# GFNet spectral filter and gated FFN on one core: a reordered opening, and the middle spectral stage two places sooner

## The chip, the cores and the metric

The kernel runs on one core of a Trainium2 chip. The metric is the device time of one execution in microseconds; before the change the median of three runs is 193.73 (193.61 to 193.73).

## The reference

The input x has 2048 rows (tokens) of 640 in bf16; the FFN's inner width is F = 1536.

```
xn  = layernorm(x)                                   # no scale, no shift
s   = irfft2(rfft2(xn) * (w_r + 1j*w_i)).astype(bf16)   # over all 2048 x 640
g   = silu((gelu(xn @ w_gate) * (xn @ w_up)) @ w_down)
out = x + s * g
```

So there are two branches out of one normalized input, a spectral filter and a gated FFN, and they meet in the last line.

## The kernel before

**Tiles.** The 2048 tokens are 16 slabs of 128; four slabs are a group of 512 (g = 0 to 3). F is 12 tiles of 128. A slab is loaded (`load_x`), its mean and variance are taken by VectorE in two halves (`bn_half`, L189) and joined (`bn_join`, L195; `stats` is both), the inverse root comes from POOL (`root`, L207, a power, behind an addition on VectorE, L205) or for slab 0 from ScalarE (`root_act`, L214, followed on L215 by a small gelu that brings in the gelu table), and VectorE normalizes in place (`norm`, L218, or in two parts, `norm_parts`). Then TensorE turns the slab (`slab_Tparts`, L994, five transposes, three and two), and the turned slab is copied out of PSUM (L995), the first part by VectorE and the second by ScalarE. Slab 2 is turned by TensorE with one copy by ScalarE, and slabs 4 to 15 by DMA (`slab_T`, L532 and L539); for slabs 4 to 7 ScalarE normalizes (`norm_act`, L461) by a product that POOL prepares (`shift`, L456).

**FFN.** For one tile t and columns c0 to c1, `ffn_piece` (L826) does five matmuls with Wg, then gelu on ScalarE (L837), and five with Wu, then the product on VectorE (L839). PSUM has two banks for gate results and two for up results (`bank`), used in turn.

**The order is written out by hand.** The list `back` has 144 places, one after the other on TensorE. Group 0 has 16 opening places for tiles 0 to 7 (first slab by slab, then with 256 columns at a time), the eight places of tiles 8 to 11 with all 512 columns, and 12 places of the down projection. Groups 1 and 2 have 24 FFN places and 12 places of `product` (six matmuls of 128x320 each); group 3 has 24 FFN places and 12 down places. `plan[s]` holds what is issued behind the matmuls of place s, by `put(s, function, ...)`: statistics, norms, building of constants (`inv_consts` and `inv_rest`, L313 and L318; the phase tables on POOL, L334 to L374 and L386), and the spectral branch.

**The spectral branch.** Forward: folds on VectorE, `slab_S1` (L555) and `slab_D`, slab by slab from place 30 to 56, written to ZDR in DRAM. Middle: `s2_step` in 11 bursts from place `sb` = 67 on, with B loaded from ZDR (L603), a first transform (px, L628), the multiplication by the weights (L644), a second one (pu, L657), sorting by ScalarE and VectorE (L672), and writes to UDR. Inverse: from `sb` + 24 on, the loads of V, `slab_S1i`, `slab_Di`, and the combination with the FFN's result (`group_*`, `finish`). All of these places are worked out from `sb`.

**The opening.** SP's queue loads in this order: X 0, X 1, Wu 0:2, Wu 2:4, X 2, Wu 4:6, X 3, Wg and Wu 6:8, X 4:8, the weights 8:12 and the rest. ScalarE's queue loads Wg 0:2, 2:4 and 4:6 (L231, L232). TensorE runs 21 warm-up matmuls on ones (`warm_pe`, L588), the transposes of slab 0, two warm-ups more, and then place 0. VectorE does the statistics of slab 0 and of slab 1, and then the norm of slab 0.

Of the kernel before, what the change touches and what calls it, by code (L numbers as in the profile page):

```python
# [10 lines left out]
BF16 = mybir.dt.bfloat16  # L11
INT32 = mybir.dt.int32
ACT = mybir.ActivationFunctionType
ALU = mybir.AluOpType
P = 128
# [17 lines left out]
def kernel(  # L33
# [39 lines left out]
    with tc.manual_schedule():  # L73
        build(nc, locals())


def build(nc, env):
    consts, big, wts, work, psA, psB = (env[k] for k in ("consts", "big", "wts", "work", "psA", "psB"))
    ZDR, UDR, X, Wg, Wu, Wd, W1, W2 = (env[k] for k in ("ZDR", "UDR", "X", "Wg", "Wu", "Wd", "W1", "W2"))
# [3 lines left out]
    def load_x(n0, n, eng=nc.sync):  # L83
        eng.dma_start(out=X[:, n0:n0 + n, :], in_=xv[:, n0:n0 + n, :])

    def load_w(k, t0, t1, eng=nc.sync):
        f0, f1 = t0 * P, t1 * P
        eng.dma_start(out=(Wg, Wu)[k][:, :, f0:f1], in_=(wgv, wuv)[k][:, :, f0:f1])

    def load_gu(t0, t1):  # L90
        for k in range(2):
            load_w(k, t0, t1)

    load_x(0, 1)
    load_x(1, 1)
    load_w(1, 0, 2)
    load_w(1, 2, 4)
    load_x(2, 1)
    load_w(1, 4, 6)
    load_x(3, 1)  # L100
    load_gu(6, 8)
    load_x(4, 4)
    load_gu(8, 12)
    load_x(8, 4)
# [32 lines left out]
    UT = consts.tile([P, NT, 512], BF16, name="UT")  # L137
# [8 lines left out]
    def slot(k, *shape):  # L146
        return XG[:, k, :].rearrange("p (a b) -> p a b", b=shape[-1])
# [25 lines left out]
    def c1(name, dt=FP32):  # L173
        return consts.tile([P, 1], dt, name=name)

    done = set()
    mva = {}
    rstd = {}
    rall = {}
    nmr = {}  # L180
    xnT = {}
# [4 lines left out]
    def bn_half(n1, k):  # L186
        if k == 0:
            st_n[n1] = work.tile([P, 2, nc.vector.BN_STATS_DIM], FP32, tag="st", bufs=3, name="st")
        nc.vector.bn_stats(out=st_n[n1][:, k, :], in_=X[:, n1, 320 * k:320 * k + 320])  # L189

    def bn_join(n1):
        g = n1 // 4
        if g not in mva:
            mva[g] = work.tile([P, 4, nc.vector.BN_AGGR_DIM], FP32, tag="mva", bufs=2, name=f"mva{g}")
        nc.vector.bn_aggr(out=mva[g][:, n1 % 4, :], in_=st_n[n1])  # L195
# [6 lines left out]
    def root(n0, n):  # L202
        m = mva[n0 // 4][:, n0 % 4:n0 % 4 + n, :]
        ve = work.tile([P, 4], FP32, tag="ve", name="ve")[:, 0:n]
        nc.vector.tensor_scalar(out=ve, in0=m[:, :, 1], scalar1=1e-5, scalar2=None, op0=ALU.add)  # L205
        r = work.tile([P, 4], FP32, tag="rst", bufs=4, name="rst")[:, 0:n]
        nc.gpsimd.tensor_tensor(out=r, in0=ve, in1=mhalf[:, 0:n], op=ALU.pow)  # L207
        rall[n0] = r
        for k in range(n):
            rstd[n0 + k] = r[:, k:k + 1]  # L210

    def root_act(n1):
        rstd[n1] = c1("rst0")
        nc.scalar.activation(out=rstd[n1], in_=mva[n1 // 4][:, n1 % 4, 1:2], func=ACT.Abs_reciprocal_sqrt, bias=eps)  # L214
        nc.scalar.activation(out=warm, in_=negpi, func=ACT.Gelu_apprx_tanh)  # L215

    def norm(n1, c0=0, c1_=D):
        nc.vector.tensor_scalar(out=X[:, n1, c0:c1_], in0=X[:, n1, c0:c1_], scalar1=mva[n1 // 4][:, n1 % 4, 0:1],  # L218
                                scalar2=rstd[n1], op0=ALU.subtract, op1=ALU.mult)
        if c1_ == D:  # L220
            done.add(("n", n1))
# [6 lines left out]
    eps = c1("eps")  # L228
    nc.vector.memset(eps, 1e-5)
    nc.scalar.activation(out=warm, in_=eps, func=ACT.Abs_reciprocal_sqrt)  # L230
    for t in (0, 2, 4):  # L231
        load_w(0, t, t + 2, nc.scalar)  # L232
    b_0, b_1 = c1("b_0"), c1("b_1")
    nc.vector.memset(b_0, 320.0)
    nc.vector.memset(b_1, 0.0)
# [92 lines left out]
    stats(0)  # L328
    bn_half(1, 0)
    root_act(0)  # L330

    def tinv_phase(h):
# [251 lines left out]
    def warm_pe(n):  # L584
        if not warm_bank:
            warm_bank.append(bank(0))
        for _ in range(n):
            nc.tensor.matmul(warm_bank[0][:, 0:256], lhsT=ones[:, 0:P], rhs=ones, start=True, stop=True)  # L588
# [230 lines left out]
    def bank(k):  # L819
        return psA.tile([P, 512], FP32, tag="gu"[k], name="ps" + "gu"[k])  # L820

    cur = {}

    ges = {}

    def ffn_piece(g, t, k, c0, c1_):  # L826
        for j in range(c0 // P, c1_ // P):
            assert ("T", 4 * g + j) in done
        ps = bank(k)[:, c0:c1_]
        WT = (Wg, Wu)[k]  # L830
        for c in range(5):
            nc.tensor.matmul(ps, lhsT=WT[:, c, t * P:(t + 1) * P], rhs=xnT[g][:, c, c0:c1_],  # L832
                             start=(c == 0), stop=(c == 4))
        flush()
        if k == 0:
            ges[t] = work.tile([P, 512], BF16, tag="ge", bufs=3, name="ge")[:, c0:c1_]
            nc.scalar.activation(out=ges[t], in_=ps, func=ACT.Gelu_apprx_tanh)  # L837
        else:
            nc.vector.tensor_tensor(out=UT[:, t, c0:c1_], in0=ps, in1=ges[t], op=ALU.mult)  # L839

    def ffn_part(g, t, h):
        for k in range(2):
            ffn_piece(g, t, k, h * 256, h * 256 + 256)

    def ffn_half(g, t, k):
        ffn_piece(g, t, k, 0, 512)
# [8 lines left out]
    def flush():  # L855
        now = put_off[:]
        del put_off[:]
        for f in now:
            f()
# [109 lines left out]
            if t == NT - 1:  # L969
                gated(g, j, k, ph)  # L970

    def ffn_slab(j, tk):
        for t, k in tk:
            ffn_piece(0, t, k, j * P, j * P + P)

    GG, UU = ((0, 0), (1, 0)), ((0, 1), (1, 1))

    def run(*items):
        for it in items:
            it[0](*it[1:])  # L980

    PARTS = ((0, 3), (3, 5))

    def norm_parts(n1):
        for a, b in PARTS:
            norm(n1, a * P, b * P)

    def slab_Tparts(n1):
        if n1 == 0:
            xnT[0] = slot(0, 5, 512)  # L990
        for (a, b), ev in zip(PARTS, (nc.vector.tensor_copy, nc.scalar.copy)):
            pt = psB.tile([P, 5, P], BF16, tag="b")
            for c in range(a, b):
                nc.tensor.transpose(out=pt[:, c, :], in_=X[:, n1, c * P:(c + 1) * P], identity=ident)  # L994
            ev(out=xnT[0][:, a:b, n1 * P:n1 * P + P], in_=pt[:, a:b, :])  # L995
        done.add(("T", n1))

    NP = 8
    STR = (1, 2)
    back = [(run, (ffn_slab, 0, GG), (norm_parts, 1), (slab_Tparts, 1), (vt_iota, 1), (ffn_slab, 0, UU),  # L1000
             (inv_consts, 0), (inv_consts, 1)),
            (run, (ffn_slab, 1, GG + UU), (stats, 2), (root, 2, 1))]
    for h in range(2):
        for t in range(0 if h else 2, NP):
            back.append((ffn_part, 0, t, h))
        if h == 0:
            back[-1] = (run, (ffn_piece, 0, NP - 1, 0, 0, 256), (slab_Tparts, 3), (ffn_piece, 0, NP - 1, 1, 0, 256))
    for g in range(4):
        for t in range(NP if g == 0 else 0, NT):
            for k in range(2):  # L1010
# [10 lines left out]
    def put(s, *item):  # L1021
        plan[s].append(item)

    put(1, inv_rest)
    put(2, norm, 2)
    put(3, bn_half, 3, 0)
    put(4, bn_half, 3, 1)
    put(4, bn_join, 3)
    put(4, root, 3, 1)
    put(4, slab_T, 2, 1)  # L1030
    put(5, norm, 3)
    for g in range(5):
        put(3 + g, ft_v, g)
        put(8 + g, ft_v, 5 + g)
# [73 lines left out]
    put(z_end, load_B2)  # L1108
    for k in range(2):
        put(TURN + k, mg_turn, k)  # L1110
    sb = 67
    AT = (0, 3, 5, 7, 9, 11, 13, 15, 17, 19, 21)
    for b in range(len(BURSTS)):
        put(sb + AT[b], s2_step, b)
# [9 lines left out]
    for i, (n0, n) in enumerate(DG):  # L1124
        a = vs0 + 6 * i
# [3 lines left out]
        d = a + (7 if n == 3 else 4)  # L1129
# [3 lines left out]
        for k in range(n):  # L1133
            put(min(d + 8 + k, LAST), finish, n0 + k)

    warm_pe(21)
    bn_half(1, 1)
    bn_join(1)
    root(1, 1)
    norm_parts(0)  # L1140
    slab_Tparts(0)
    warm_pe(2)

    put(5, phase_const)

# [35 lines left out]
```

## Time and profile before

| what | value |
|---|---|
| median of 3 runs | 193.73 us (193.61 to 193.73) |
| the profiled execution | 193.65 us |
| its span | 191.9 us |
| granted TensorE clock | 1.0 |
| first matmul of the FFN | 6.84 us |
| first matmul of place 8 (second half of group 0's columns) | 16.50 us |
| first matmul of the middle stage | 89.60 us |
| end of the last matmul | 188.67 us |

All times of the trace are counted from the start of the span. A row of the timeline is the start, the busy time of a group of like instructions, the engine, the line, the operation, what it writes and reads, and in brackets the idle time before it with what ended it. A row of the waits is the engine, the tile and line that waited, what it waited for, and then the total, the count and the longest wait. A row of the windows has the window, its length, and the busy time of PE, PEld, DVE, ACT and POOL, with the granted clock, the share of DMA and GB/s. PE is TensorE, DVE is VectorE, ACT is ScalarE, POOL is GpSimd, SP is the engine that issues most DMAs. A row of the DMA issues ends with the size and the us from issue to landing.

### The profile page before, as it was taken

Reading aid. Unit: us, or ns where it says so; the run is one execution under the profiler, and the core shown is the slowest. Engines: PE = TensorE matmul, PEld = TensorE weight load, DVE = VectorE, ACT = ScalarE, POOL = GpSimd, SP = SyncE. Lnnn points to the kernel's source line nnn. Section 1 sums busy time; section 2 is a strip of 40 time slices with the busy share of each in tenths; the row PEclk is TensorE's granted clock in tenths of the full one; section 3 lists DMA queues with packets and bytes.
Section 4 is the critical chain, followed back from the end, with each engine's and each line's share of the span. In section 5 each row is a group of like instructions: output and inputs, shape, how many; then the busy total and the mean of one; then the engine's idle time right before and its main releaser. Section 6 shows DMA issues by size and latency. Waiting matters only on the chain.

```text
span 191.9 us, 4068 instructions
## 1 busy us (share of the span) xinstructions
PE 186.1 (97%) x1453; PEld 115.6 (60%) x1469; DVE 150.9 (79%) x364; ACT 131.9 (69%) x241; POOL 53.9 (28%) x91
## 2 busy tenths in 40 slices
PE   7999999999999999999999999999999999999993
PEld 5788854677655665566543334347775555556772
DVE  6787889899799889846978677685445898888973
ACT  4658557957878778536697878634989776876622
POOL 4458768999040200000000000002030134150400
PEclk9999999999999999999999999999999999999999
DMA  6999999948889994249996444149900084778842
GB/s 164 300 329 360 370 332 170 172 99 318 178 165 191 211 300 120 78 111 230 223 108 123 106 103 103 42 107 273 266 5 0 0 117 111 152 153 213 121 174 62
DMA packets 39700, 32.43 MB, mean 169 GB/s; under 512 B 12928, under 2 KB 37760, under 8 KB 39552
## 3 DMA queue, kind: packets, MB, share of 16 engines
q1 hardware_dynamic: 35888, 27.91, 58.6%
q0 software_dynamic: 1824, 3.28, 9.4%
q10 hardware_dynamic: 1968, 0.98, 1.9%
q8 instruction: 11, 0.18, 0.4%
q14 instruction: 9, 0.07, 0.1%
HBM read 19.03 MB, written 7.88 MB: 140 GB/s over the span
## 4 chain that ended last, share of the span: by engine, by line
PE 95%; DMA 2%; DVE 1%; issue 1%; SPq 0%; ACT 0%
PE psu L832 27%; PE psg L832 27%; PE psg L967 7%; PE psg L933 7%; PE psu L967 6%; PE psu L933 5%; PE pu L657 2%; PE pd L762 2%; PE pv L735 2%; PE pz L555 2%; PE pd L573 2%; PE px L628 2%; DMA X<-in_A_x_dram 2%; PE pt L994 1%; PE pd L575 1%
## 5 line engine op out<-in xcount | busy, mean ns | idle before, releaser
L832 PE MATMUL psu<-XG,Wu 128*128 128x512 bf16 (+2 forms) x284 | 60.4, 342 | 0.5 <-issue 0.3
L832 PE MATMUL psg<-XG,Wg 128*128 128x512 bf16 (+2 forms) x280 | 60.1, 341 | 0.6
L839 DVE TENSOR_TENSOR UT<-psu,ge 128x512 bf16<-128x512 f32 (+2 forms) x58 | 34.4, 594 | 13.6 <-PE psu L832 8.1
L837 ACT ACTIVATE ge<-psg 128x512 bf16<-128x512 f32 (+2 forms) x58 | 30.3, 523 | 21.3 <-PE psg L832 20.6
L832 PEld LDWEIGHTS <-Wu 128*128 128x128 bf16 x290 | 25.9, 98 | 20.9 <-issue 3.4
L832 PEld LDWEIGHTS <-Wg 128*128 128x128 bf16 x290 | 26.5, 98 | 18.8 <-issue 0.2
L967 PEld LDWEIGHTS <-UT 128*128 128x128 bf16 x204 | 19.1, 98 | 6.9
L813 POOL DMA_DIRECT2D VY<-in_A_x_dram x12 | 10.6, 964 | 26.2 <-ACT W L737 10.5
L713 POOL COPY vr<-VY 128x128 bf16<-128x128 bf16 x2 | 0.6, 291 | 60.2 <-DMA VY<-UDR 60.2
L644 DVE TENSOR_TENSOR RZ<-xs,W 128x960 bf16<-128x960 bf16 (+2 forms) x22 | 13.3, 647 | 4.4 <-ACT xs L640 4.4
L967 PE MATMUL psg<-Wd,UT 128*128 128x320 bf16 (+1 forms) x108 | 15.7, 290 | 0.0
L578 ACT CAST RZ<-pd 128x660 bf16<-128x660 f32 x16 | 11.3, 706 | 5.2 <-PE pd L575 5.2
L189 DVE BATCH_NORM_STATS2 st<-X 128x6 f32<-128x320 bf16 x32 | 14.0, 476 | 0.6 <-DMA X<-in_A_x_dram 0.4
L933 PEld LDWEIGHTS <-UT 128*128 128x128 bf16 x120 | 11.4, 98 | 4.8 <-issue 0.4
L967 PE MATMUL psu<-Wd,UT 128*128 128x320 bf16 (+1 forms) x96 | 13.9, 293 | 0.0
L737 ACT CAST W<-pv 128x640 bf16<-128x640 f32 x16 | 11.1, 691 | 3.1 <-PE pv L735 3.1
L763 ACT ACTIVATE W<-pd 128x640 bf16<-128x640 f32 x16 | 11.3, 706 | 1.5 <-PE pd L762 1.5
L557 ACT CAST GEN<-pz 128x640 bf16<-128x640 f32 x16 | 11.2, 698 | 1.2 <-PE pz L555 1.2
L672 ACT CAST RX<-pu 128x480 bf16<-128x480 f32 (+3 forms) x22 | 10.8, 489 | 1.1 <-DVE RX L672 0.3
L640 ACT CAST xs<-px 128x960 bf16<-128x960 f32 (+2 forms) x11 | 10.3, 933 | 0.0
L207 POOL TENSOR_TENSOR rst<-ve,mhalf 128x1 f32<-128x1 f32 (+1 forms) x6 | 5.5, 913 | 11.5 <-DVE ve L205 11.5
L933 PE MATMUL psg<-X,UT 128*128 128x320 bf16 x48 | 7.8, 300 | 0.0
(202 smaller groups left out, 302.1 us busy)
## 6 DMA issues: line engine op xcount, KB each, us to landing
ZDR<-RZ SPq DMA_DIRECT2D x16, 160.5 KB, 4.1
UDR<-RX SPq DMA_DIRECT2D x10, 240.8 KB, 3.1
B<-ZDR SPq DMA_DIRECT2D x8, 240.8 KB, 5.2
W<-UDR SPq DMA_DIRECT2D x2, 963.0 KB, 9.1
X<-in_A_x_dram SPq DMA_DIRECT2D x3, 640.0 KB, 10.3
Wd<-in_B_w_down_dram SPq DMA_DIRECT2D x1, 1920.0 KB, 14.6
VY<-in_A_x_dram POOLq DMA_DIRECT2D x12, 160.0 KB, 4.3
out_dram<-VY SPq DMA_DIRECT2D x12, 160.0 KB, 2.8
```

The costliest lines, as they stand in the source:

```text
L189: nc.vector.bn_stats(out=st_n[n1][:, k, :], in_=X[:, n1, 320 * k:320 * k + 320])
L557: nc.scalar.copy(out=Zt[n1], in_=pz)
L578: nc.scalar.copy(out=zd.rearrange("p c (q e) -> p c q e", e=10), in_=pd[:, :, 0:330].rearrange("p c (e q) -> p c q e", q=33))
L644: nc.vector.tensor_tensor(out=pp[-1], in0=xs, in1=WT[:, :, h0:h0 + n, l0:l0 + w], op=ALU.mult)
L672: copy(out=out, in_=src)
L737: nc.scalar.copy(out=vs, in_=pv)
L763: nc.scalar.activation(out=parts(eobuf, i, 5)[:, :, n1 - DG[i][0], :], in_=pd, func=ACT.Copy, scale=(2.0 if n1 // 4 in BY_SILU else 1.0) / ...
L832: nc.tensor.matmul(ps, lhsT=WT[:, c, t * P:(t + 1) * P], rhs=xnT[g][:, c, c0:c1_], start=(c == 0), stop=(c == 4))
L837: nc.scalar.activation(out=ges[t], in_=ps, func=ACT.Gelu_apprx_tanh)
L839: nc.vector.tensor_tensor(out=UT[:, t, c0:c1_], in0=ps, in1=ges[t], op=ALU.mult)
L933: nc.tensor.matmul(ps, lhsT=lhs[:, t, :], rhs=rhs[:, t, :], start=(t == 0 and i in (0, 1, 3)), stop=(t == 5), skip_group_check=i in (2, 4, ...
L967: nc.tensor.matmul(ph, lhsT=UT[:, t, j * P:(j + 1) * P], rhs=Wd[:, t, c0:c1_], start=(t == 0), stop=(t == NT - 1))
```

## The change

Five things change.

1. The loads. Wg's three loads leave ScalarE's queue; SP's queue now has X 0, X 1, Wg 0:4, Wu 0:2, Wu 2:4, X 2, Wg 4:8, X 3, Wu 4:8, X 4:8 and the rest as before.
2. The beginning. The norm, the transposes and the copies of slab 0 come ahead of the second half of slab 1's statistics. The root of slab 1 is ScalarE's, and the load of the gelu table comes behind it. Both copies of slabs 0 and 1 are VectorE's. There are 19 warm-ups ahead of slab 0's transposes and 4 behind them.
3. The opening places. `ffn_multi` replaces `ffn_part` and `ffn_slab`: four tiles of one slab go into one bank (20 matmuls of 128 columns, then one gelu or one product over all), later two tiles of 256 columns. The transposes of slabs 1, 2 and 3 stand between the two halves of an up place (places 1, 6 and 7). There are 16 opening places as before.
4. What is put where: the statistics, roots and norms of slabs 2 and 3 come a place or so sooner; `inv_consts` and `inv_rest` come at place 7 instead of 0 and 1.
5. `sb` is 65 instead of 67, so the middle stage, the loads of V, the inverse stage and the finish come two places sooner. `slab_T` of slabs 12 to 15 stays at 65, 68, 71 and 74.

```diff
     load_x(0, 1)
     load_x(1, 1)
+    load_w(0, 0, 4)
     load_w(1, 0, 2)
     load_w(1, 2, 4)
     load_x(2, 1)
-    load_w(1, 4, 6)
+    load_w(0, 4, 8)
     load_x(3, 1)
-    load_gu(6, 8)
+    load_w(1, 4, 8)
     load_x(4, 4)
...
     def root_act(n1):
-        rstd[n1] = c1("rst0")
+        rstd[n1] = c1("rst%d" % n1)
         nc.scalar.activation(out=rstd[n1], in_=mva[n1 // 4][:, n1 % 4, 1:2], func=ACT.Abs_reciprocal_sqrt, bias=eps)
+
+    def gelu_table():
         nc.scalar.activation(out=warm, in_=negpi, func=ACT.Gelu_apprx_tanh)
...
-    for t in (0, 2, 4):
-        load_w(0, t, t + 2, nc.scalar)
...
+    def ffn_multi(k, t0, n, c0, c1_, half=None):
+        w = c1_ - c0
...
+        if half in (None, 0):
+            cur["m"] = bank(k)[:, 0:n * w].rearrange("p (t w) -> p t w", w=w)
+        ps = cur["m"]
+        WT = (Wg, Wu)[k]
+        for i in range(n) if half is None else range(half * n // 2, (half + 1) * n // 2):
+            for c in range(5):
+                nc.tensor.matmul(ps[:, i, :], lhsT=WT[:, c, (t0 + i) * P:(t0 + i + 1) * P], rhs=xnT[0][:, c, c0:c1_],
+                                 start=(c == 0), stop=(c == 4))
+        if half == 0:
+            return
+        flush()
...
-        for (a, b), ev in zip(PARTS, (nc.vector.tensor_copy, nc.scalar.copy)):
+        for (a, b), ev in zip(PARTS, (nc.vector.tensor_copy, nc.scalar.copy if n1 > 1 else nc.vector.tensor_copy)):
...
-    back = [(run, (ffn_slab, 0, GG), (norm_parts, 1), (slab_Tparts, 1), (vt_iota, 1), (ffn_slab, 0, UU),
-             (inv_consts, 0), (inv_consts, 1)),
-            (run, (ffn_slab, 1, GG + UU), (stats, 2), (root, 2, 1))]
-    for h in range(2):
-        for t in range(0 if h else 2, NP):
-            back.append((ffn_part, 0, t, h))
-        if h == 0:
-            back[-1] = (run, (ffn_piece, 0, NP - 1, 0, 0, 256), (slab_Tparts, 3), (ffn_piece, 0, NP - 1, 1, 0, 256))
+    back = [(run, (ffn_multi, 0, 0, 4, 0, P), (vt_iota, 1)),
+            (run, (ffn_multi, 1, 0, 4, 0, P, 0), (slab_Tparts, 1), (ffn_multi, 1, 0, 4, 0, P, 1)),
+            (run, (ffn_multi, 0, 0, 4, P, 256)),
+            (run, (ffn_multi, 1, 0, 4, P, 256))]
+    for h, k, t0 in ((0, 0, 4), (0, 0, 6), (0, 1, 4), (0, 1, 6)) + tuple((1, k, t) for t in (0, 2, 4, 6) for k in range(2)):
+        back.append((ffn_multi, k, t0, 2, 256 * h, 256 * h + 256))
+    back[6] = (run, (ffn_multi, 1, 4, 2, 0, 256, 0), (slab_T, 2, 1), (ffn_multi, 1, 4, 2, 0, 256, 1))
+    back[7] = (run, (ffn_multi, 1, 6, 2, 0, 256, 0), (slab_Tparts, 3), (ffn_multi, 1, 6, 2, 0, 256, 1))
...
-    put(1, inv_rest)
-    put(2, norm, 2)
-    put(3, bn_half, 3, 0)
-    put(4, bn_half, 3, 1)
-    put(4, bn_join, 3)
-    put(4, root, 3, 1)
-    put(4, slab_T, 2, 1)
-    put(5, norm, 3)
+    put(1, stats, 2)
+    put(1, root, 2, 1)
+    put(2, bn_half, 3, 0)
+    put(2, bn_half, 3, 1)
+    put(3, norm, 2)
+    put(3, bn_join, 3)
+    put(3, root, 3, 1)
+    put(5, norm_parts, 3)
+    for part in range(2):
+        put(7, inv_consts, part)
+    put(7, inv_rest)
...
-    sb = 67
+    sb = 65
...
-    warm_pe(21)
+    warm_pe(19)
+    norm_parts(0)
+    slab_Tparts(0)
+    warm_pe(4)
     bn_half(1, 1)
     bn_join(1)
-    root(1, 1)
-    norm_parts(0)
-    slab_Tparts(0)
-    warm_pe(2)
+    root_act(1)
+    gelu_table()
+    norm_parts(1)
```

More of the change, by code (lines that the diff above doesn't have):

```diff
@@ L839, in ffn_piece @@
             nc.vector.tensor_tensor(out=UT[:, t, c0:c1_], in0=ps, in1=ges[t], op=ALU.mult)
-    def ffn_part(g, t, h):
-        for k in range(2):
-            ffn_piece(g, t, k, h * 256, h * 256 + 256)
+    def ffn_multi(k, t0, n, c0, c1_, half=None):
+        w = c1_ - c0
+        for j in range(c0 // P, c1_ // P):
+            assert ("T", j) in done
+        if half in (None, 0):
[9 more added lines that the diff above has]
+        flush()
+        if k == 0:
+            ge = work.tile([P, 512], BF16, tag="ge", bufs=3, name="ge")[:, 0:n * w].rearrange("p (t w) -> p t w", w=w)
+            ges[t0, c0] = ge
+            nc.scalar.activation(out=ge, in_=ps, func=ACT.Gelu_apprx_tanh)
+        else:
+            nc.vector.tensor_tensor(out=UT[:, t0:t0 + n, c0:c1_], in0=ps, in1=ges[t0, c0], op=ALU.mult)
     def ffn_half(g, t, k):
@@ L970, in down_third @@
                 gated(g, j, k, ph)
[L972 to L976, printed above, removed]
     def run(*items):
```

## The prediction

> **What bounds the kernel now.** I read the page first: the shares of the engines, then the chain that ended last.
>
> ```profile
> span 191.9 us, 4068 instructions
> PE 186.1 (97%) x1453; PEld 115.6 (60%) x1469; DVE 150.9 (79%) x364; ACT 131.9 (69%) x241; POOL 53.9 (28%) x91
> GB/s 164 300 329 360 370 332 170 172 99 318 178 165 191 211 300 120 78 111 230 223 108 123 106 103 103 42 107 273 266 5 0 0 117 111 152 153 213 121 174 62
> PE 95%; DMA 2%; DVE 1%; issue 1%; SPq 0%; ACT 0%
> ```
>
> TensorE is busy 97% of 191.9 us and is 95% of the chain. Next the waits of that engine, largest first (total us, count, longest):
>
> ```profile
> PE psg L588 <- DVE eps L229: 1.2, 1, 1.2
> PE pt L994 <- DVE X L218: 0.3, 1, 0.3
> PE psu L832 <- issue: 0.3, 2, 0.2
> ```
>
> No wait behind the opening reaches 0.3 us. So a stage moved in the middle can't win anything by itself: its matmuls only change places in a full stream. What can be won lies ahead of the first real matmul, while 21 warm-ups (L588) fill the time. The timeline of the opening:
>
> ```profile
> 1.18 4.55 PE L588 MATMUL psg<-GEN 128*128 128x256 bf16 x21 [1.18 <-DVE eps L229]
> 3.13 0.89 DVE L189 BATCH_NORM_STATS2 st<-X 128x6 f32<-128x320 bf16 x2 [0.45 <-DMA X<-in_A_x_dram]
> 4.05 0.21 DVE L195 BATCH_NORM_AGGREGATE mva<-st 128x2 f32<-128x12 f32 x1
> 4.29 0.29 ACT L214 ACTIVATE rst<-mva,eps 128x1 f32<-128x1 f32 x1 [2.08 <-DVE mva L195]
> 4.38 0.89 DVE L189 BATCH_NORM_STATS2 st<-X 128x6 f32<-128x320 bf16 x2
> ...
> 5.62 0.63 DVE L218 TENSOR_SCALAR X<-X,mva,rst 128x384 bf16<-128x384 bf16 x2
> 6.05 0.54 PE L994 MATMUL pt<-ident,X 128*128 128x128 bf16 x5 [0.32 <-DVE X L218]
> 6.43 0.36 DVE L995 COPY XG<-pt 128x384 bf16<-128x384 bf16 x1 [0.18 <-PE pt L994]
> 6.63 0.37 ACT L995 COPY XG<-pt 128x256 bf16<-128x256 bf16 x1 [0.53 <-PE pt L994]
> 6.84 0.76 PE L832 MATMUL psg<-XG,Wg 128*128 128x128 bf16 x10
> ...
> 16.50 0.60 PE L832 MATMUL psg<-XG,Wg 128*128 128x256 bf16 x4
> ```
>
> Slab 0's scale is ready at 4.58 (ACT, 4.29 + 0.29), but VectorE does slab 1's statistics first and normalizes slab 0 only at 5.62. The first gate matmul follows at 6.84. At 16.50 the second half of group 0's columns (place 8) begins; I use it as a milestone, since the same columns have been multiplied by then in both kernels.
>
> **The opening, step by step.** In the changed kernel only one half of slab 1's statistics (0.89/2 = 0.45) stands between slab 0's aggregation and its norm. The aggregation ends at 4.26, the half at 4.70 if X of slab 1 is there (the same row in before starts at 4.38, so 4.83 at the latest). I take the norm at 4.75 instead of 5.62. The 21 warm-ups are 4.55/21 = 0.217 apart, so after 19 TensorE is free at 1.18 + 19 x 0.215 = 5.26 at the latest; the last ones overlap, and I take 5.21. Before, the transposes came 0.43 behind the norm's start (5.62 to 6.05), which gives 5.18. So both meet at 5.2. The transposes then run at the warm-ups' pace, half a 256-wide one (0.11) each, not at the 0.057 of the full clock, which costs 0.1 to 0.15: copy one at 5.74, done 6.10. The second copy is now also on VectorE, right behind, done at about 6.30. The first three matmuls of a tile need only the first copy; the first gate matmul therefore starts at about 6.17 to 6.20, and the fourth one waits for no more than some hundredths, as it did before. That is 0.69 to 0.65 sooner.
>
> From there to place 8 there is the same work in both: 16.50 - 6.84 = 9.66 of TensorE. The four-tile places have 40 more 128-wide matmuls and 20 fewer of 256; at 0.76/10 busy per matmul, which overlap, I allow 0.04. Place 8 comes at about 15.85 instead of 16.50: **-0.65**. Bounds: -0.55 (norm at 4.83, transposes late) to -0.72. Two edits hide behind this: slab 1's root on ACT and the gelu table load behind it (0.29 + 1.3) end near 8.7, and the four tiles of a slab fill one bank with 20 matmuls, so the first gelu is wanted only after 20 x 0.055 = 1.1 from 6.17, and its bank only at the second next place, after 9. Cost nothing, up to 0.1 if the table load is late.
>
> **Loads.** All weights now come in one queue, in order of need. Bytes of X and weights up to the last piece for the first eight tiles (Wu 4:8): 4 x 160 + 4 x 640 KB = 3.28 MB, the same as before up to Wu 6:8.
>
> ```profile
> 8.85 0.37 SPq L88 DMA_DIRECT2D Wu<-in_B_w_up_dram  x1
> ...
> Wu<-in_B_w_up_dram SPq DMA_DIRECT2D x1, 320.0 KB, 5.4
> ```
>
> Before, that last piece was issued at 8.85 and landed 5.4 later, at 14.25, with X 4:8 and more already running beside it. The GB/s row above (slices of 4.8 us) gives 0.79 MB by 4.8 and 2.23 MB by 9.6; the missing 1.05 MB at 329 GB/s take 3.2, so 12.8 (and that rate counts other loads too). With the 365 of slices four and five for the pieces with longer rows: 12.3. The first matmul on Wu 4:8 is due 2.9 ahead of place 8 (four tiles of 5 x 0.114, two sets of transposes of 0.3): 15.85 - 2.87 = 13.0. The other pieces by the same row: Wg 0:4 (0.98 MB) 5.45, due 6.2; Wu 0:2 6.55, due 7.3; Wu 2:4 7.65, due 8.1; Wg 4:8 10.3, due 10.9. So nothing waits, with margins of 0.2 to 0.8. Value 0; bounds 0 and 14.25 - 13.0 = 1.25.
> A rule of the Trainium skill speaks against my 12.3: its page "DMA: Bandwidth & Descriptors", section "Specifications", gives 512 B as the smallest transfer for line rate, by which rows of 1 KB would win nothing over those of 512 B; the sum would then stand on 12.8 alone, or later. No row here separates the two lengths at one load.
>
> **POOL's constants.** inv_consts and inv_rest move from places 0 and 1 to place 7, so behind the product of the tile before place 8. The rows of POOL, of ACT and of the matmul that waits for them:
>
> ```profile
> 11.84 0.26 POOL L323 TENSOR_SCALAR y_e<-pb,x_e 128x1 f32<-128x1 f32 x1
> ...
> 13.57 0.26 POOL L323 TENSOR_SCALAR k_m<-pb,y_m 128x1 f32<-128x1 f32 x1
> 15.50 2.38 POOL L334 TENSOR_SCALAR GEN<-GEN,u,ph_t 128x1024 int32<-128x1024 int32 x2 [0.67 <-DVE ph_t L282]
> ...
> 21.21 1.49 POOL L374 TENSOR_TENSOR GEN<-GEN 128x660 f32<-128x660 f32 x1
> 25.27 1.04 POOL L207 TENSOR_TENSOR rst<-ve,mhalf 128x4 f32<-128x4 f32 x1 [2.57 <-DVE ve L205]
> 26.81 0.92 ACT L461 ACTIVATE X<-X,nmr,rst 128x640 bf16<-128x640 bf16 x1 [1.54 <-POOL nmr L456]
> 27.64 0.58 ACT L837 ACTIVATE ge<-psg 128x512 bf16<-128x512 f32 x1
> ...
> 29.55 0.60 PE L832 MATMUL psg<-XG,Wg 128*128 128x512 bf16 x2
> ```
>
> The six operations take 11.84 to 13.83, 1.99. Behind them the table phases take 15.50 to 22.70, 7.2. Then POOL was idle for 2.57 before the root of slabs 4 to 7 (25.27), and 1.5 later ACT's norm_act starts (26.81; it waited 1.54 for POOL even before). Behind norm_act on ACT stands the gelu of tile 8 (27.64 to 28.22), and its bank is used again by the gate at 29.55.
> After: y_e starts about 1.05 behind place 8, 16.9; + 1.99 + 7.2 = 26.1 for the root, instead of 25.27 - 0.65 = 24.62. norm_act at 26.1 + 1.54 = 27.64, the gelu ends 0.83 + 0.58 later, 29.05; the gate is due at 29.55 - 0.65 = 28.9, with a semaphore's 0.05. **+0.2.** Bounds: 0 (POOL's operations take the space between them, 0.3 less) and +0.5.
>
> POOL's lag lives on in the middle stage's phases, whose last links are:
>
> ```profile
> 34.41 0.37 POOL L386 TENSOR_SCALAR vg<-kr,n1x,php 128x16 int32<-128x16 int32 x1
> ...
> 37.47 1.96 POOL L386 TENSOR_SCALAR vg<-kr,n1x,phs 128x16 int32<-128x16 int32 x1
> ...
> 42.46 0.17 DVE L425 TENSOR_SCALAR vg<-vg 128x128 int32<-128x128 int32 x1
> ...
> 45.91 0.39 PE L555 MATMUL pz<-Tfwd,RX 128*128 128x128 bf16 x4
> ```
>
> One operation of this shape took 0.37 here and 1.96 there, beside VectorE's folds. POOL reaches them about 1.4 later against the matmuls; the mask at 42.46 then holds VectorE and, behind it, ACT's copies for the slab of 45.91. I take +0.05, bounds 0 and 0.4.
> The Trainium skill, "SBUF — State Buffer", section "SBUF: two separate sides", says that VectorE and GpSimd share a port pair as an exclusive lock, on which the loser blocks for the whole instruction; the 0.37 against 1.96 agrees. If such a lock caught inv_rest beside VectorE's products, each hit would add up to 1.6 to POOL's chain. That is the third rival below.
>
> **The middle stage and all behind it two places sooner.** Its loads of B are tied to slabs that don't move, so their margin shrinks; the rest moves as one.
>
> ```profile
> 82.94 6.26 SPq L603 DMA_DIRECT2D B<-ZDR  x10
> B<-ZDR SPq DMA_DIRECT2D x1, 240.8 KB, 4.1
> 89.60 0.40 PE L628 MATMUL px<-B,MG 64*64 64x160 bf16 x5
> 135.00:140.00 5.00, 5.00 (x53) 3.86 (x52) 1.44 (x3) 4.99 (x12) 0.02 (x1) 1.00 0.73 216
> ```
>
> The first burst stands at 89.60; a place there is a product or two of six 128x320 matmuls, and I estimate 1.6 for the two places, so 88.0. Its loads are the first two of the ten, which are issued 0.63 apart from 82.94; the second, issued at about 83.5, landed 4.1 later (the second row), at 87.6. The margin falls from 2.0 to 0.4; the later bursts need one more load each, a place or two later. The V loads behind keep their distance, the inverse slabs come two places sooner into a stretch (135 to 140) where ACT is busy 4.99 of 5.00. I take +0.05 for each of load and inverse stage, and nothing for the two transposes that SP now does ahead of the UDR writes. Bounds -0.1 to +0.5 together.
>
> **Sum.** 193.65 (profiled execution; the median of the runs is 193.73, so take 0.08 as the spread) - 0.65 + 0.2 + 0.05 + 0.1 = **193.3**. The tail behind the last matmul stays. About 0.2% (0.39) is what a measurement of this kernel can tell from no change.
>
> **Rivals.**
> 1. *Nothing is given back* (POOL's chain has 0.3 more slack than I think, and the stage moves free): 193.65 - 0.65 to -0.72 = 192.9 to 193.0. For it: POOL comes 26.1 - 24.62 = 1.48 late against a slack of 29.55 - 28.22 = 1.33 on the bank, a near thing. Chance 0.15.
> 2. *The single queue is late, slower than before.* Wu 4:8 lands at 14.25 as the same bytes did before; TensorE stands 1.25 at place 6: 193.3 + 1.25 = 194.5. It decides from a landing of 13.8 (193.3 + 0.8 = 194.1). For it: the same bytes. Against it: 14.25 was reached with X 4:8 and the next weights already under way beside that piece, which with one order by need stand behind it, and the page's rate gives 12.8. Chance 0.15.
> 3. *POOL or ACT eats the gain*: one hit of 1.6 on POOL's chain, or ACT's full stretch, takes 0.3 to 0.7 more: 193.6 to 194.0. For it: 1.96 in place of 0.37, ACT at 4.99 of 5.00. Chance 0.25, a fifth of it above 194.1.
> 4. *The middle move is the point and wins by itself*: needs a stall in the waits above; there is none. Below 192.9, chance under 0.03, left in the first.
>
> **Chances.** Forecast (193.1 to 193.5) 0.45, two thirds of it below 193.34. Faster by over 0.2%: 0.30 + 0.15 = 0.45; within: 0.15 + 0.20 = 0.35; slower: 0.15 + 0.05 = 0.20. The range 192.9 to 194.2 leaves out most of the second rival and the ends of the first and third.
>
> **What would show it.** First gate matmul at 6.2 and place 8 near 15.85: the opening is right; if place 8 comes later, the wait is on Wu or on the copies. The wait of the matmul near 28.9 on ACT of about 0.2, behind norm_act waiting for POOL's nmr: the constants. A wait of px on B or of the inverse slabs on ACT: the middle stage. A PE stream whose gaps are all as short as now, with a time above 193.5, would make the prediction wrong altogether.

## The result, and the profile after

The changed kernel takes 196.02 us (median of six runs), the kernel before 193.85 beside it; the ratio is 1.0113, with an interval of 1.0098 to 1.0128. It is slower by 1.1%, or 2.2 us, where the forecast had 193.3 and a range up to 194.2.

One run of the changed kernel (329.99 us, at a granted clock of 0.563) and one of the kernel before (327.87 us) are left out of the ratio, and since the first of these was the profiled one, the rows "after" are from a second profile (e1 below, 195.54 us, clock 1.0). Its page: span, engines, and the chain that ended last.

```profile
span 193.7 us, 4074 instructions
PE 185.7 (96%) x1473; PEld 115.7 (60%) x1489; DVE 151.1 (78%) x358; ACT 130.1 (67%) x230; POOL 53.3 (28%) x90
...
PE 86%; POOL 6%; DMA 3%; issue 1%; SPq 1%; DVE 1%; ACT 0%; ACTq 0%; DVEq 0%
```

TensorE does the same work (185.7 against 186.1), but the chain, which was 95% TensorE, now holds 6% of POOL and 3% of DMA. That is two stalls, and the waits of TensorE name both:

```profile
PE psg L589 <- DVE eps L232: 1.2, 1, 1.2
PE psg L852 <- DMA Wg<-in_B_w_gate_dram: 1.2, 1, 1.2
PE psg L833 <- ACT ge L838: 1.0, 1, 1.0
```

The first row was there before; the second (gate, first slab, on its weights) and the third (a gate bank on a gelu) are new. The timeline of the opening:

```profile
4.59 0.63 DVE L221 TENSOR_SCALAR X<-X,mva,rst 128x384 bf16<-128x384 bf16 x2
...
5.03 0.54 PE L1007 MATMUL pt<-ident,X 128*128 128x128 bf16 x5 [0.27 <-DVE X L221]
...
5.41 0.56 DVE L1008 COPY XG<-pt 128x384 bf16<-128x384 bf16 x2 [0.18 <-PE pt L1007]
...
7.15 1.29 PE L852 MATMUL psg<-XG,Wg 128*128 128x128 bf16 x20 [1.15 <-DMA Wg<-in_B_w_gate_dram]
...
17.11 0.60 PE L852 MATMUL psg<-XG,Wg 128*128 128x256 bf16 x4
```

The norm of slab 0 starts at 4.59 instead of 5.62 and its copies are done at 5.97 (5.41 + 0.56): the chain that the change set out to shorten is a second shorter. But the first gate matmul stands idle for the weights until 7.15, and place 8 comes at 17.11, 0.61 later than before instead of 0.65 sooner. Ahead of the end, the chain has the same down group in both kernels, before (the first row) and after (the second):

```profile
187.99 0.68 PE psg L967 x12
```

```profile
189.71 0.68 PE psg L986 x12
```

That is 1.72 later. 0.61 of it stands at place 8 already; the rest, 1.11, is the wait for the gelu near 31 (0.97 by the row of the waits). The middle and inverse stages add nothing. Behind the last matmul the changed kernel takes 3.35 and the kernel before 3.21, so the span grows by 1.85.

### The profile page after: what moved, and what is told of

It reads as the page before. It is cut to its first block, busy times and chain, and to the rows that moved or that the text cites. A ratio compares the mean times of both kernels' runs of the same rounds, so it can differ in the third digit from the quotient of the medians.

```text
span 327.8 us, 4074 instructions
## 1 busy us (share of the span) xinstructions
PE 319.2 (97%) x1473; PEld 162.8 (50%) x1489; DVE 153.3 (47%) x358; ACT 133.5 (41%) x230; POOL 46.8 (14%) x90
## 4 chain that ended last, share of the span: by engine, by line
PE 96%; DMA 2%; issue 1%; SPq 0%; DVE 0%; ACT 0%
PE psu L833 23%; PE psg L833 23%; PE psg L986 7%; PE psg L952 7%; PE psu L986 7%; PE psu L952 5%; PE psu L852 5%; PE psg L852 5%; PE pu L658 2%; PE pv L736 2%; PE pz L556 2%; PE pd L763 2%; PE pd L574 2%; DMA Wg<-in_B_w_gate_dram 2%; PE px L629 1%
## 5 line engine op out<-in xcount | busy, mean ns | idle before, releaser
L833 PE MATMUL psg<-XG,Wg 128*128 128x512 bf16 x190 | 82.5, 582 | 1.8 <-issue 0.9
L833 PE MATMUL psu<-XG,Wu 128*128 128x512 bf16 x194 | 82.0, 577 | 0.8 <-issue 0.6
L840 DVE TENSOR_TENSOR UT<-psu,ge 128x512 bf16<-128x512 f32 x40 | 27.7, 692 | 88.5 <-PE psu L833 86.2
L838 ACT ACTIVATE ge<-psg 128x512 bf16<-128x512 f32 x40 | 23.9, 598 | 66.4 <-PE psg L833 66.4
L833 PEld LDWEIGHTS <-Wu 128*128 128x128 bf16 x200 | 24.6, 131 | 41.1 <-issue 40.2
L833 PEld LDWEIGHTS <-Wg 128*128 128x128 bf16 x200 | 25.2, 131 | 39.0 <-issue 38.5
L986 PEld LDWEIGHTS <-UT 128*128 128x128 bf16 x204 | 26.1, 131 | 19.9 <-issue 1.2
L986 PE MATMUL psg<-Wd,UT 128*128 128x320 bf16 (+1 forms) x108 | 26.3, 420 | 0.0
L952 PEld LDWEIGHTS <-UT 128*128 128x128 bf16 x120 | 15.7, 135 | 12.0 <-issue 1.9
L852 PE MATMUL psg<-XG,Wg 128*128 128x256 bf16 (+1 forms) x100 | 16.8, 351 | 1.2 <-DMA Wg<-in_B_w_gate_dram 1.2
L852 PE MATMUL psu<-XG,Wu 128*128 128x256 bf16 (+1 forms) x100 | 17.5, 354 | 0.0
L852 PEld LDWEIGHTS <-Wg 128*128 128x128 bf16 x100 | 11.6, 132 | 5.0 <-DMA Wg<-in_B_w_gate_dram 1.5
L852 PEld LDWEIGHTS <-Wu 128*128 128x128 bf16 x100 | 12.0, 136 | 3.4
## 6 DMA issues: line engine op xcount, KB each, us to landing
X<-in_A_x_dram SPq DMA_DIRECT2D x3, 640.0 KB, 10.3
Wd<-in_B_w_down_dram SPq DMA_DIRECT2D x1, 1920.0 KB, 13.8
```

The costliest lines, as they stand in the source:

```text
L852: nc.tensor.matmul(ps[:, i, :], lhsT=WT[:, c, (t0 + i) * P:(t0 + i + 1) * P], rhs=xnT[0][:, c, c0:c1_], start=(c == 0), stop=(c == 4))
L952: nc.tensor.matmul(ps, lhsT=lhs[:, t, :], rhs=rhs[:, t, :], start=(t == 0 and i in (0, 1, 3)), stop=(t == 5), skip_group_check=i in (2, 4, ...
L986: nc.tensor.matmul(ph, lhsT=UT[:, t, j * P:(j + 1) * P], rhs=Wd[:, t, c0:c1_], start=(t == 0), stop=(t == NT - 1))
```

## The experiments

Theory A: the weights of the first tiles land late on the one queue. Theory B: POOL's constants, moved behind place 7, hold norm_act and so a gelu. Theory C: the two places of the middle stage cost time. Ratios are to the kernel before, run beside each.

**e1, the changed kernel again** (no edit).

> The changed kernel once more, for a profile at the full granted clock (the first profile of it was taken at 0.563). Theory A, late weights: Wg 0:4 lands near 7.8 as in the first profile, because three of its sixteen parts come 0.8 to 1.8 behind the others; the first gate matmul starts near 7.8 instead of the forecast 6.2, and place 8 near 17.5 instead of 15.85, so 1.0 of the 2.2 lost is lost there. Theory B, the constants on POOL: place 8 comes near 16.0 and TensorE waits 1 or more at the gates of tiles 9 to 11 (29 to 32 us), behind norm_act and nmr. Theory C, the middle stage: the waits stand behind 88 us, on px for B or on the inverse slabs for ACT.

195.54. A and B both hold, C doesn't: no wait behind 88 us. The issue rows of the first gate pieces, before (the first row, ScalarE's queue) and after (the second), end with KB and us to landing:

```profile
Wg<-in_B_w_gate_dram ACTq DMA_DIRECT2D x1, 320.0 KB, 4.3
```

```profile
Wg<-in_B_w_gate_dram SPq DMA_DIRECT2D x1, 640.0 KB, 5.5
```

The issue is 0.45 later and the piece twice as large: it lands at 7.1 instead of 5.5. The trace has sixteen landings for each load, and the gate starts right behind the last of them (landing 7.11 and start 7.15 here; 7.41 and 7.46 in e3; 6.81 and 6.85 in e4). For this load they are (us):

```
5.55 5.81 5.91 5.92 5.97 5.99 6.00 6.01 6.02 6.07 6.08 6.24 6.30 6.33 6.86 7.11
```

By stretches of one microsecond (the last column is GB/s), after and then before, the loads of after also begin more slowly:

```profile
3.00:4.00 1.00, 1.00 (x7) 0.69 (x6) 0.89 (x2) 0.00 (x0) 0.76 (x1) 1.00 0.86 131
4.00:5.00 1.00, 0.76 (x7) 0.43 (x5) 0.98 (x4) 0.29 (x1) 0.00 (x0) 1.00 0.93 287
```

```profile
3.00:4.00 1.00, 1.00 (x7) 0.67 (x6) 0.87 (x2) 0.00 (x0) 0.75 (x1) 1.00 0.97 297
4.00:5.00 1.00, 1.00 (x7) 0.67 (x6) 0.84 (x4) 0.69 (x2) 0.00 (x0) 1.00 1.15 342
```

With ScalarE's queue beside SP's, 297 GB/s were moved between 3 and 4; with SP's alone, 131. The queue is not all of it, for the first piece is also larger: on SP's queue alone with a first piece of 320 KB (e11) it was 247. Of the sixteen landings, eleven are there by 6.08; the last two come 0.8 and 1.0 later, and in the six loads behind it, up to Wu 4:8, the last two trail by as much. In e1, e3, e4 and e7, which have this order on one queue, the last landing is at 7.11, 7.41, 6.81 and 7.16.

**e2, the loads of before in the changed kernel.**

```diff
-    load_w(0, 0, 4)
...
-    load_w(0, 4, 8)
+    load_w(1, 4, 6)
     load_x(3, 1)
-    load_w(1, 4, 8)
+    load_gu(6, 8)
...
+    for t in (0, 2, 4):
+        load_w(0, t, t + 2, nc.scalar)
```

> The changed kernel with the loads of the kernel before: Wg in three pieces on ScalarE's queue beside SP's. Theory A: the first gate matmul comes back to 6.2 to 6.4 and the kernel gains 1.0 to 1.6, to 194.4 to 195.0. Theories B and C: within 0.3 of the changed kernel, 196.0.

195.81, ratio 1.0119 (1.0103 to 1.0134): no gain. The first gate matmul did come sooner (Wg 0:2 lands at 5.12; until 6.59 TensorE was busy with the four warm-ups behind the transposes, 0.21 apart in this profile and 0.11 in e1), but the four-tile places now wait for the second piece:

```profile
6.59 0.92 PE L853 MATMUL psg<-XG,Wg 128*128 128x128 bf16 x10
8.03 0.68 PE L853 MATMUL psg<-XG,Wg 128*128 128x128 bf16 x9 [0.52 <-DMA Wg<-in_B_w_gate_dram]
```

After ten matmuls (tiles 0 and 1) tile 2 wants Wg 2:4, which lands at 7.99. Place 8 is at 17.16, the same as with the one queue. So A is not "one queue against two" alone. With four tiles of one slab ahead of the next slab, all four tiles' weights are due within a microsecond.

**e3, the middle stage back** (sb = 67).

> The changed kernel with the middle stage and all behind it at the old places (sb = 67). Theory C: gains 1.0 or more, to 195.0 or less, and the waits behind 88 us go. Theories A and B: within 0.2 of 196.0; my own forecast put 0.1 on this move.

196.36, ratio 1.0142 (1.0123 to 1.016): no gain, so C falls. In its profile Wg landed at 7.41 and place 8 came at 17.42; from place 8 to the last matmul it took 173.15, against 173.05 in e1.

**e4, the constants at place 3.**

```diff
-        put(7, inv_consts, part)
-    put(7, inv_rest)
+        put(3, inv_consts, part)
+    put(3, inv_rest)
```

> The changed kernel with inv_consts and inv_rest at place 3 instead of 7. Theory B: POOL's chain is early again, the wait behind norm_act near 29 to 31 us goes, gain 0.5 to 1.2. Theory A: gain 0.2 at most, as the forecast had for that term. Theory C: nothing.

194.54, ratio 1.0064 (1.0034 to 1.0094), with a wide spread: the nine runs behind the ratio go from 193.60 to 196.34. By the ratios that is 0.95 less than the changed kernel; in the profiles the way from place 8 to the last matmul takes 171.84 instead of e1's 173.05. The waits of TensorE, all that are left:

```profile
PE psg L589 <- DVE eps L232: 1.2, 1, 1.2
PE psg L852 <- DMA Wg<-in_B_w_gate_dram: 0.9, 1, 0.9
PE psu L833 <- issue: 0.3, 2, 0.2
PE psg L852 <- DVE XG L1008: 0.2, 1, 0.2
```

The wait for the gelu is gone, the one for Wg stays. B is shown. How it came about, in e1's rows of POOL, of VectorE beside it, of ScalarE and of the matmul that waits:

```profile
18.25 0.27 POOL L324 TENSOR_SCALAR y_e<-pb,x_e 128x1 f32<-128x1 f32 x1 [3.32 <-DVE x_o L273]
...
20.26 2.38 POOL L335 TENSOR_SCALAR GEN<-GEN,u,ph_t 128x1024 int32<-128x1024 int32 x2
...
23.44 3.01 POOL L373 TENSOR_SCALAR GEN<-GEN 128x660 f32<-128x660 f32 x1
26.53 1.82 POOL L375 TENSOR_TENSOR GEN<-GEN 128x660 f32<-128x660 f32 x1
28.32 1.03 POOL L208 TENSOR_TENSOR rst<-ve,mhalf 128x4 f32<-128x4 f32 x1
```

```profile
23.39 0.76 DVE L340 TENSOR_SCALAR GEN<-GEN,andm,orm 128x1024 int32<-128x1024 int32 x1
...
25.82 0.65 DVE L206 TENSOR_SCALAR ve<-mva 128x4 f32<-128x4 f32 x1
25.90 1.10 DVE L340 TENSOR_SCALAR GEN<-GEN,andm,orm 128x1024 int32<-128x1024 int32 x1
```

```profile
29.84 0.92 ACT L462 ACTIVATE X<-X,nmr,rst 128x640 bf16<-128x640 bf16 x1 [4.29 <-POOL nmr L457]
30.67 0.58 ACT L838 ACTIVATE ge<-psg 128x512 bf16<-128x512 f32 x1
```

```profile
31.29 0.81 PE L833 MATMUL psg<-XG,Wg 128*128 128x512 bf16 x3 [0.97 <-ACT ge L838]
```

The chain is the forecast's, link by link, but POOL's table phases take 20.26 to 28.35, 8.1 instead of 7.2: the two operations that took 2.45 and 1.49 before take 3.01 and 1.82. Pushed back, they meet the masks of VectorE (L340), of which one starts 0.05 ahead of the first and the other runs from 25.90 to 27.00, into the second. The profiles of e2, e3 and e11, with the constants at the same place, show the same (2.99 to 3.01, and 1.82); in those of e4 and e6 POOL's operation is the one that starts first, and there it keeps its 1.50 (e4) and 2.45 (e6) while the mask takes 1.05 instead of 0.76. The Trainium skill, "SBUF — State Buffer", section "SBUF: two separate sides", has the two engines' shared port pair as an exclusive lock for a whole instruction. The small operation of VectorE (L206) agrees: it takes 0.65 here, and 0.17 in the kernel before, and ends 0.02 behind POOL's first (26.47 and 26.45). A mask in e6 doesn't: it starts and ends inside POOL's operation. No run here moves the masks alone, so the collision is read from the trace.

**e5, sb = 65 alone on the kernel before.**

> The kernel before with sb = 65 as its only change. Theory: the middle stage two places sooner moves matmuls inside a full stream and is worth nothing, -0.1 to +0.3 (my forecast had +0.1). Rival: it wins by itself, 0.4 or more, since the changed kernel lost nothing behind 50 us and its last matmul came 0.08 sooner against the first product places.

193.88, ratio 1.0011 (1.0002 to 1.002), eleven runs. The move wins nothing by itself, and costs a tenth of a per cent. No wait of TensorE behind the opening shows in its profile.

**e6, the late constants alone on the kernel before.**

```diff
-             (inv_consts, 0), (inv_consts, 1)),
+             ),
...
-    put(1, inv_rest)
+    for part in range(2):
+        put(7, inv_consts, part)
+    put(7, inv_rest)
```

> The kernel before with inv_consts and inv_rest at place 7 as its only change. Theory: POOL's chain (1.99 for the six operations, then 7.2 to 8.1 for the table phases) comes late, norm_act waits for nmr, and one gate matmul behind place 18 waits for ACT: +0.8 to +1.2. Rival, as the forecast had it: +0.2.

194.15, ratio 1.0026 (1.0015 to 1.0037), so +0.5, between the two. POOL, VectorE beside it, and the wait:

```profile
22.53 2.45 POOL L372 TENSOR_SCALAR GEN<-GEN 128x660 f32<-128x660 f32 x1
25.07 1.50 POOL L374 TENSOR_TENSOR GEN<-GEN 128x660 f32<-128x660 f32 x1
```

```profile
22.79 1.05 DVE L339 TENSOR_SCALAR GEN<-GEN,andm,orm 128x1024 int32<-128x1024 int32 x1
...
25.23 1.35 DVE L205 TENSOR_SCALAR ve<-mva 128x4 f32<-128x4 f32 x1
26.50 0.41 DVE L839 TENSOR_TENSOR UT<-psu,ge 128x256 bf16<-128x256 f32 x1
```

```profile
26.96 0.81 PE L832 MATMUL psu<-XG,Wu 128*128 128x512 bf16 x3 [0.51 <-DVE UT L839]
```

Here the table phases kept their 7.2, and the stall of 0.5 is another one than in e1. VectorE's small operation (L205) takes 1.35 instead of 0.17, to the end of POOL's second (26.58 and 26.57); the product behind it starts at 26.50 instead of the 25.10 of the kernel before, and the up matmul waits for that product. ScalarE is no part of it: its norm_act comes at 28.20, after the stall, and its gelu ends at 29.61, ahead of the gate at 30.20, which doesn't wait. So the same meeting of POOL and VectorE costs 0.5 where POOL starts first and VectorE is held, and more in the changed kernel, where POOL is held.

**e7, the changed loads alone on the kernel before.** The diff of the loads is that of the change.

> The kernel before with the changed loads (all on SP's queue, by need) as the only change. Theory: Wg 0:4 lands at 6.8 to 7.8 by the slowest of its sixteen parts, so the first gate matmul waits 0.1 to 0.9, and Wu 0:2 at 8.0 to 8.9 instead of 7.0, so that the first up matmul (due at 7.72) waits too: +0.4 to +1.3. Rival: the loads cost nothing in an opening that begins at 6.84, within 0.2.

195.47, ratio 1.0091 (1.0076 to 1.0105). The loads alone make 1.8 of loss, more than the 0.4 to 1.3 expected, on a kernel whose opening begins at 6.84:

```profile
PE psu L831 <- DMA Wu<-in_B_w_up_dram: 1.2, 1, 1.2
PE psg L831 <- DMA Wg<-in_B_w_gate_dram: 0.4, 1, 0.4
```

```profile
14.09 0.61 PE L831 MATMUL psu<-XG,Wu 128*128 128x256 bf16 x4 [1.17 <-DMA Wu<-in_B_w_up_dram]
```

Wg 0:4 lands at 7.16 and Wu 4:8 at 14.04, where the order of tiles in that kernel wants tile 4's up weights at 12.1 (12.8 with the two waits ahead). In the changed order Wu 4:8 lands at 13.99 (e1) and doesn't stall, since the gate tiles 4 to 7 stand ahead and the opening was late already.

**e8, two queues and an order by landings.** The loads of before; inv_consts and inv_rest at places 0 and 1; `ffn_open(k, slab, half)` does two of the four tiles of `ffn_multi`, into the same bank, and the gelu or product behind the second half; and:

```diff
     norm_parts(0)
+    bn_half(1, 1)
     slab_Tparts(0)
     warm_pe(4)
-    bn_half(1, 1)
...
+    back = [(run, (ffn_open, 0, 0, 0), (ffn_open, 1, 0, 0), (vt_iota, 1)),
+            (run, (slab_Tparts, 1), (ffn_open, 0, 0, 1), (ffn_open, 0, 1, 0)),
+            (run, (ffn_open, 1, 1, 0), (ffn_open, 0, 1, 1)),
+            (run, (ffn_open, 1, 0, 1), (ffn_open, 1, 1, 1))]
```

> The changed kernel with the loads of before on two queues, inv_consts and inv_rest at places 0 and 1 as before, slab 1's second half of statistics ahead of slab 0's copies, and the matmuls of the first two slabs in the order of the pieces' landings (tiles 0 and 1 of gate and up, slab 1's transposes, then gate of tiles 2 and 3, up last). Theory: the first gate matmul at 6.2 to 6.6, waits of 0.2 to 0.5 on Wu 0:2 and Wg 2:4, place 8 at 16.0 to 16.4, no wait behind norm_act: 193.1 to 193.5, 0.1 to 0.6 under the kernel before. Rival: the opening is bound by the weights' bytes whatever the order, place 8 at 16.5 or later: 193.6 to 194.0.

194.88, ratio 1.0068 (1.0052 to 1.0083), above the ranges of theory and rival. The rival's place 8 holds: the first gate matmul comes at 5.91, nearly a second sooner than before, and place 8 at 17.06 all the same. Between them TensorE loses 0.6 on Wu 0:2 (landing 7.06), 0.25 on Wg 2:4 (8.15), 0.25 on Wg 6:8 (12.85), and 0.3 on slab 3's copy at place 8.

**e9 and e10, the changed kernel mended, with sb = 67 and 65.**

```diff
-    load_w(0, 0, 4)
-    load_w(1, 0, 2)
+    load_w(0, 2, 4)
     load_w(1, 2, 4)
...
+    for k in range(2):
+        load_w(k, 0, 2, nc.scalar)
```

with the constants at places 0 and 1 and slab 1's statistics as in e8, and the changed places.

> The changed kernel, mended where the runs so far put the loss, with sb = 67: Wg 0:2 and Wu 0:2 on ScalarE's queue, the rest on SP's in the changed order, inv_consts and inv_rest at places 0 and 1, slab 1's second half of statistics ahead of slab 0's copies. Theory, the opening is bound by the landings: the first gate matmul at 6.0 to 6.4, waits of 0.2 to 0.6 in all on Wg 2:4 (near 7.0) and Wu 2:4 (near 8.5), place 8 at 16.2 to 16.6, no wait behind norm_act: 193.3 to 193.8. Rival: with the two losses mended the forecast holds, place 8 at 15.9, 193.0.

> The same with sb = 65 as in the changed kernel. Theory: 0.0 to 0.3 more than with 67 (65 alone on the kernel before cost 0.11%). Rival: the move wins where the opening is right, 0.2 or more less.

e9 194.82, ratio 1.0051 (1.0033 to 1.0069); e10 194.19, ratio 1.0024 (1.0012 to 1.0036), the best of those that compute all. Mending wins 1.2 (e9) and 1.8 (e10) of the 2.2, but neither beats the kernel before, and the time that e9's theory gave (193.3 to 193.8) is missed by 1.0. What is won is POOL's part: no gelu is waited for any more, but place 8 comes at 17.05 in e9, hardly sooner than in e1. e10's profile, of the slowest of its twelve runs, has it at 17.69, with X 0 landing at 4.16 where the other profiles have 2.9 to 3.2, so it says little of the others. On sb the theory was wrong and its rival right: here 65 is 0.6 better, though the two intervals just overlap. e9's profile shows a wait for it,

```profile
PE pv L737 <- POOL vr L717: 0.5, 1, 0.5
```

the first inverse slab on its V load. In the kernel before, the second of the two V loads lands 0.8 ahead of the first inverse matmul (132.30 and 133.13), in e10 1.5 ahead (131.12 and 132.60). With sb = 67 this margin is 0.8 (before), 1.1 (e3) and 0.3 (e9, the wait), with 65 it is 1.0 (e5), 1.7 (e1) and 1.5 (e10). So the earlier stage seems to buy margin for a late transfer rather than time; three profiles on each side are little for that. In e5's profile the last matmul ends 0.4 sooner than before, but what follows it takes 3.63 instead of 3.21; whether that is where e5's 0.1% comes from stays open.

**e11, Wg 0:4 in two pieces, one queue.**

```diff
-    load_w(0, 0, 4)
+    load_w(0, 0, 2)
+    load_w(0, 2, 4)
```

> The changed kernel with Wg 0:4 as two loads of 320 KB, still one behind the other on SP's queue. Theory: what is slow is the first weights on one queue, in all of whose sixteen parts two or three fall behind; Wg 0:2 lands near 6.0 to 6.8, Wg 2:4 near 7.1 as the whole did, place 8 near 17.0 and the time within 0.4 of the changed kernel. Rival: the 640 KB piece with its longer rows is what falls behind; then both halves land by 6.2 and the time falls by 0.6 to 1.0.

195.20, ratio 1.0081 (1.006 to 1.0102), profile 195.22. Wg 0:2 lands at 5.80 and the gate starts at 6.09, as the forecast had it; Wg 2:4 lands at 6.92, Wu 0:2 at 8.06, and place 8 comes at 16.85. A smaller first piece moves most of the wait to the next pieces: of the 1.06 that the gate starts sooner, 0.26 is left at place 8. By the ratios the time is 0.6 lower than the changed kernel's, which was the rival's size, but the intervals touch. The rival's landings (both halves by 6.2) didn't come, so the length of the rows is not the main cause; the position of the bytes in one queue fits the rows better.

**e12, without the up weights in the opening.** The up matmuls of the first eight tiles of group 0 read Wg, so the result is another one; Wu 0:8 is loaded after the last X, and X 3 comes ahead of Wg 4:8. The rest is as in e10.

```diff
-        WT = (Wg, Wu)[k]
+        WT = Wg
```

> Leaves out the up weights of the first eight tiles of group 0: their up matmuls read Wg instead of Wu, so that no load of Wu stands in the opening (it comes after the last X). For the rest the changed kernel with Wg 0:2 on ScalarE's queue, inv_consts and inv_rest at places 0 and 1, slab 1's second half of statistics ahead of slab 0's copies, sb = 65. Theory, the opening is bound by the landings: with half of the bytes gone it runs as forecast, first gate matmul at 6.0 to 6.3, place 8 at 15.8 to 16.3 (with the 0.3 for slab 3's copy), 193.0 to 193.4, under the kernel before. Rival: something else holds the opening, the chain of slab 1 or the banks; then place 8 stays at 16.9 or later and the time at 194.0 or more.

193.42, ratio 0.9996 (0.9987 to 1.0006): level with the kernel before. With half of the bytes gone no load holds TensorE any more:

```profile
PE psg L588 <- DVE eps L230: 1.2, 1, 1.2
PE psu L832 <- issue: 0.3, 2, 0.2
PE psg L851 <- DVE XG L1007: 0.2, 1, 0.2
```

The first gate matmul starts at 6.26 and place 8 at 16.25:

```profile
16.25 0.38 PE L851 MATMUL psg<-XG,Wg 128*128 128x256 bf16 x2 [0.15 <-DVE XG L1007]
```

Against e10 this shows that the weights' landings were worth 0.5 by the ratios (0.8 by the medians). Against the forecast's 15.85 it shows what the reordered opening brought where no weights hold it: 0.25, not 0.65. Even that is not clear of the spread: in e5, with the opening of before, place 8 stood at 16.21. Of the rest, 0.1 went at the start and 0.3 at place 8, where slab 3's copy on VectorE stands behind a product:

```profile
15.24 0.69 DVE L861 TENSOR_TENSOR UT<-psu,ge 128x512 bf16<-128x512 f32 x1 [0.30 <-ACT XG L547]
15.84 0.35 DVE L1007 COPY XG<-pt 128x384 bf16<-128x384 bf16 x1
```

The product of two tiles at once takes 0.69 where one of 256 columns took 0.42, and the copy waits for all of it. Why it starts no sooner than 15.24 is open; the wait that the profile names, slab 2's copy on ScalarE, is not one of its inputs.

## Why the prediction was wrong

- **What bounds the kernel** held: TensorE, and nothing to win behind the opening by moving work (e5, e3).
- **The opening, as a chain of engines**, held to about 0.3: norm at 4.75 forecast and 4.59 measured, copies done at 6.30 and 5.97, first gate matmul possible at 6.17 to 6.20, and 5.91 (e8), 6.09 (e11), 6.26 (e9 and e12) where no weights held it. In e2 it came at 6.59, behind warm-ups at the slow pace. On the way from there to place 8 the forecast saw no wait; slab 3's copy cost 0.3 in e12.
- **The loads are the step that failed**: "So nothing waits, with margins of 0.2 to 0.8. Value 0". In e1 all five pieces landed 1.4 to 1.7 after the forecast, and 0.8 to 1.2 after they were due by it:

| piece | forecast | due | last landing in e1 |
|---|---|---|---|
| Wg 0:4 | 5.45 | 6.2 | 7.11 |
| Wu 0:2 | 6.55 | 7.3 | 8.25 |
| Wu 2:4 | 7.65 | 8.1 | 9.33 |
| Wg 4:8 | 10.3 | 10.9 | 11.66 |
| Wu 4:8 | 12.3 | 13.0 | 13.99 |

The forecast took for the landing the time at which a mean rate has moved the bytes, and two things were missing in it. The rate was that of the kernel before, with two queues, and the bytes came more slowly: eleven of the sixteen landings of Wg 0:4 were there by 6.08, just ahead of the due time but 0.6 after the forecast. And the matmul waits for the last of the sixteen, which is 0.8 to 1.5 behind most of the others (e4, e3). I also set the bounds on the last piece (Wu 4:8, 0 to 1.25) and gave the first pieces none. Instead of -0.65 the opening gave +0.61: 1.26 of the miss. The second rival had the price, and also the landing of Wu 4:8 (13.8 or later), but its stall was to stand at place 6. It came at place 0, and with the late start the up matmuls of tile 4 begin only at 14.37 and no longer wait. The 12.3 doesn't follow from its own rate either: 9.6 + 1.05/0.365 is 12.5.

- **POOL's constants**: the mechanism was right, the size was not. Forecast +0.2, measured 1.1 (the gate of 29.55 comes at 31.29, 1.74 later, of which 0.61 stood at place 8). 0.1 is y_e's start (1.14 behind place 8 instead of 1.05), 0.9 is the table phases at 8.1 instead of 7.2. That is the third rival in kind, with VectorE's masks in the place of its products. I had carried a duration over to a place where another engine's work stands beside it.
- **The middle stage and all behind it**: forecast +0.1 for loads and inverse stage, found about -0.1 by the traces (171.84 from place 8 to the start of the last matmul in e4, e5, e8 and e10, against 171.94 before) and +0.2 by the times of e5. No wait of px on B, none of the inverse slabs on ScalarE. The +0.05 for the middle stage's phases wasn't seen either.
- **The sum**: -0.65 + 0.2 + 0.15 was forecast, +0.61 + 1.11 + 0 measured in one profile, and 0.14 more behind the last matmul, where the forecast had no change. The median is 0.5 above that profiled run; the spread of the Wg landings (6.81 to 7.41) may cover a part, and the rest is not traced.

## What to carry to other kernels

A chain that ends in a load is due when the last of the load's sixteen parts lands, not when the mean rate has moved its bytes: take the landing of a like piece from the trace and give the first pieces the widest bounds. Shortening the head of a kernel wins only as much as its next-latest input allows; list for each piece of data when it lands and when it is first wanted, and put the smallest difference beside the gain (here 0.2 for Wg 4:6 already in the kernel before: landing 11.37, first use 11.58). Work moved later on an idle engine changes its neighbours, and so its duration, as well as its start.

## What the runs showed of the hardware

- The sixteen landings of one load spread by 0.3 in one case (the second X slab in e1, 3.23 to 3.52) and by 1.7 in another (Wg 0:4 in e3, 5.72 to 7.41). The lag of the last two stayed the same in the six loads queued behind Wg 0:4 (0.8 and 1.0 in e1, up to Wu 4:8). The trace doesn't tell which part a landing belongs to, so that it is the same parts each time is inferred from the equal lags.
- The warm-ups' pace changed at different times in runs of like kernels, at a granted clock of 1.0 in all: the matmuls of 256 columns on ones went from 0.213 apart to 0.110 at about 4.0 in e1 and 5.8 in e12, and in e2 the gate matmuls of 128 columns went from 0.107 to 0.056 at 7.0. A single profile's opening can be some tenths early or late by this.
- Where an operation of POOL and one of VectorE met in e1 and e6, the one that started second was the one that took longer: POOL's 3.01 instead of 2.45 behind a mask (e1), VectorE's 1.35 instead of 0.17 behind POOL (e6).
